# Attention and two gated MLPs on one core: a leaky rectifier in the weight conversion, and another order of the stages

## The chip, the cores and the metric

The kernel runs on one core of a Trainium2 chip. The time is that of one execution on the device, in microseconds, and what counts is the median of several runs. The profile is one execution recorded by the hardware; its own time stands beside it.

## The reference

The inputs are drawn as float32, but the weights and activations must keep nearly float32 accuracy. There are four batches of 12 heads, 448 positions and 64 features.

```
q, k   = rmsnorm(q) * g_q, rmsnorm(k) * g_k
attn   = softmax(q @ k.T / 8) @ v                 # per head
x      = attn, heads side by side                 # 1792 x 768
x      = ((x @ w_a) * (x @ w_b)) @ w_out          # 768 -> 1536 -> 768
h      = x @ w2_in                                # 768 -> 2048
g      = max(h, 0) + alpha * min(h, 0)            # alpha: one per column
out    = g @ w2_out                               # 2048 -> 768
```

## The kernel before

The work is split by batch and by stage. For each batch b there is the attention, and four stages: `a` (both products with `w_a` and `w_b`, 24 blocks of 18 matmuls), `y` (with `w_out`, 12 blocks), `h` (with `w2_in`, 16 blocks) and `o` (with `w2_out`, 24 blocks of 12 matmuls). All matmuls of a stage are 128x128 by 128x448 in float16. A number is carried as two float16 halves, a high and a low part, and three products are added, which gives 18 matmuls for six tiles (`prod`).

The order of the 16 stages is one written-out list, `stages` (L584). Attention of batch 0 runs alone, in float32, ahead of everything. Attention of batches 1 to 3 is cut into 21 steps each (`att_steps`): a step takes two blocks of query rows through scores, softmax (L417, L434), the split of the probabilities into halves (L477, L478) and a transposing DMA, and every 3.5 steps the product with v. The dictionary `RATE` (L883) says how many steps are laid between the blocks of a stage; whatever of batch b is still missing ahead of stage `a` of b is done there (`while done < ...`).

The weights come as pairs of 32-bit words of float64 numbers. Each block of weights is used once per batch. On its first use a block is loaded raw (`w_load`, L618), turned to float32 (`w_convert`), given a scale by a power of two from the sum of its squares (`w_scale`, `total`, `power`), split into halves (`w_split`, L684 and L685) and written to a scratch area in HBM (L688); later uses read it from there (L614). There are 76 such conversions: 24 in a, 12 in y, 16 in h, 24 in o. The list `STEPS` (L692) says how many blocks each of the four operations runs ahead of the block being multiplied.

`w_convert` works on the high words: ScalarE writes their absolute value times 2^-112 (L633), VectorE shifts the bits left by 3 (L634), puts the sign bit back (L637) and adds the top bits of the low word (L640); for `o` the inverse scale of `h` is multiplied in (L646). `w_scale` takes the squares (L666), sums them over the partitions by a small matmul with ones (the tile `tot`) and makes the scale.

Stage `h` evacuates a block as Relu(ps * cg) and Relu(-ps * cg) on ScalarE (L830, L831), adds alpha times the second (L832), copies to float16 (L836) and takes the rest as the low half (L837). Stages `a` and `y` do their own split (L739, L740) right away if the next stage is of the same batch; otherwise it is done piece by piece between the blocks of the following stages (`after`, `tasks`).

All activations live in a pool of 35 slots of one size. DMAs are issued on SyncE's queue (SP) in program order. A scheduler lays out the instructions of each engine from their order in the program and their dependences; a few are pinned by `keep_in_program_order`.

Of the kernel before, what the change touches and what calls it, by code (L numbers as in the profile page):

```python
# [8 lines left out]
F32 = mybir.dt.float32  # L9
F16 = mybir.dt.float16  # L10
# [3 lines left out]
AF = mybir.ActivationFunctionType  # L14
ALU = mybir.AluOpType
# [4 lines left out]
def attention_gated_mlps_kernel(  # L20
# [15 lines left out]
    nc = tc.nc  # L36
    B, H, S, D = q.shape
    DM, DF = w_a.shape
    DF2 = w2_in.shape[1]
    KD, KF, KF2 = DM // 128, DF // 128, DF2 // 128  # L40
    NP = H // 2
    NI = S // 64
    KB = 4
    KP = S // KB
    SLOTS = 35

    const = ctx.enter_context(tc.tile_pool(name="const", bufs=1))
    acts = ctx.enter_context(tc.tile_pool(name="acts", bufs=1))
# [5 lines left out]
    ob_p = ctx.enter_context(tc.tile_pool(name="ob", bufs=2))  # L54
    in_p = ctx.enter_context(tc.tile_pool(name="in", bufs=2))
    one_p = ctx.enter_context(tc.tile_pool(name="one", bufs=1))
    two_p = ctx.enter_context(tc.tile_pool(name="two", bufs=2))
    sm_p = ctx.enter_context(tc.tile_pool(name="sm", bufs=4))
# [6 lines left out]
    def slot(name):  # L65

        return slot_p.tile([128, 2, S], F16, tag="slot", name=name)
# [8 lines left out]
    kT0 = [kT0[:, i] for i in range(2)]  # L76
    kd0 = acts.tile([128, 2 * KB * D], F32, name="kd0")
    k16 = acts.tile([KP, 2, 2 * KB, 2, D], F16, name="k16")
    p16 = [acts.tile([128, 2, KB, 128], F16, name=f"p16_{i}") for i in range(3)]
    stat = [acts.tile([128, 2, NI + 2 * KB], F32, name=f"stat{i}") for i in range(2)]  # L80

    ident = const.tile([128, 128], F32, name="ident")
# [7 lines left out]
    gi = const.tile([128, 1], F32, name="gi")  # L90
    esc = const.tile([128, 1], F32, name="esc")
    al = const.tile([128, KF2], F32, name="al")
    alb = const.tile([128, KF2], F32, name="alb")
    cg = const.tile([128, 1], F32, name="cg")
    icg = const.tile([128, 1], F32, name="icg")
    ncg = const.tile([128, 1], F32, name="ncg")
    ssv = const.tile([KP, B, NP], F32, name="ssv")
    ssab = const.tile([128, 2, KF], F32, name="ssab")
    sx, ix, sab, iab, sy, iy, cum = [
# [12 lines left out]
    def power(total, s, i):  # L112


        n = total.shape[1]
        h = sm_p.tile([128, 4], I32, tag="pw", name="pw")[:, 0:n]
        nc.vector.tensor_scalar(
            h, total.bitcast(I32), 1, 0x7F800000, op0=ALU.logical_shift_right, op1=ALU.bitwise_and
        )
        nc.vector.tensor_scalar(  # L120
            s.bitcast(I32), h, -1.0, float(205 << 23), op0=ALU.mult, op1=ALU.add
        )
        nc.vector.tensor_scalar(i.bitcast(I32), h, 1.0, float(49 << 23), op0=ALU.mult, op1=ALU.add)

    def total(cols, n, groups=1):

        ps = ps_x.tile([128, 512], F32, tag="x", name="tot")
        p = cols.shape[0]
        mm(ps[:, 0:n], ones[:p], cols, True, True)
        if n == groups:  # L130
            return ps[:, 0:n]
        t = sm_p.tile([128, 4], F32, tag="tot", name="tots")[:, 0:groups]
        nc.vector.reduce_sum(
            out=t, in_=ps[:, 0:n].rearrange("p (g k) -> p g k", g=groups), axis=AX.X
        )
        return t
# [24 lines left out]
    def setup2():  # L161
        nc.gpsimd.dma_start(out=gbc, in_=g_q.rearrange("(o d) -> o d", o=1).broadcast_to([128, D]))
        nc.gpsimd.dma_start(out=gkb, in_=g_k.rearrange("(o d) -> o d", o=1).broadcast_to([128, D]))
        nc.gpsimd.dma_start(out=al, in_=alpha.rearrange("(f p) -> p f", p=128))
        nc.gpsimd.tensor_scalar(al, al, -1.0, None, op0=ALU.mult)

    def setup3():
        tc.keep_in_program_order(
# [15 lines left out]
    def setup4():  # L184

        q = sm_p.tile([128, KF2], F32, tag="al2", name="al2")
        nc.vector.tensor_tensor(q, al, al, op=ALU.mult)
        m = sm_p.tile([128, 1], F32, tag="alm", name="alm")
        nc.vector.tensor_reduce(out=m, in_=q, axis=AX.X, op=ALU.max)
        t = total(m, 1)  # L190
        one = sm_p.tile([128, 1], F32, tag="alm", name="alo")
        nc.vector.tensor_scalar(one, t, 1.0, None, op0=ALU.max)
        power(one, cg, icg)
        nc.vector.tensor_scalar(cg, cg, 2.0 ** -31, None, op0=ALU.mult)
        nc.vector.tensor_scalar(ncg, cg, -1.0, None, op0=ALU.mult)
        nc.vector.tensor_scalar(icg, icg, 2.0 ** 31, None, op0=ALU.mult)


# [160 lines left out]
        d["qT"], d["kT"] = qT, kT  # L359

    def load_vn(b, p):
        vn = one_p.tile([KP, 2, KB, D], F32, tag="vn", name="vn")
        nc.sync.dma_start(
            out=vn, in_=v[b, 2 * p:2 * p + 2].rearrange("h (p i) d -> p h i d", i=KB)
        )
        return vn
# [151 lines left out]
    X, Y, AB, G = {}, {}, {}, {}  # L518
# [62 lines left out]
            yield fin  # L581


    stages = "a0 y0 a1 y1 h0 o0 h1 o1 a2 y2 h2 a3 o2 y3 h3 o3".split()  # L584

    CHAINS = {"a": (2 * KF, 1, KD), "y": (KD, 2, KF // 2), "h": (KF2, 1, KD), "o": (KD, 4, KF2 // 4)}

    GROUP = {"a": 2, "y": 1, "h": 2, "o": 1}
# [16 lines left out]
    def size(kind):  # L605
        return CHAINS[kind][2] * 128
# [17 lines left out]
    def w_convert(u):  # L624
        if u not in raws:
            return
        kind, n, part = stream[u]
        raw = raws.pop(u)
        pair = raw.bitcast(I32).rearrange("p (n t) -> p n t", t=2)
        lo, hi = pair[:, :, 0], pair[:, :, 1]  # L630
        t = wf_p.tile([128, 768], F32, tag="wf", name="wf")[:, 0:size(kind)]
        ti = t.bitcast(I32)
        nc.scalar.activation(out=t, in_=hi.bitcast(F32), func=AF.Abs, scale=2.0 ** -112)  # L633
        i = nc.vector.tensor_scalar(ti, ti, 3, None, op0=ALU.logical_shift_left)  # L634
        if u == 0:
            tc.keep_in_program_order(i)
        nc.vector.scalar_tensor_tensor(  # L637
            out=ti, in0=hi, scalar=-0x80000000, in1=ti, op0=ALU.bitwise_and, op1=ALU.bitwise_or
        )
        nc.vector.scalar_tensor_tensor(  # L640
            out=ti, in0=lo, scalar=29, in1=ti, op0=ALU.logical_shift_right, op1=ALU.bitwise_or
        )
        if kind == "o":
            k = CHAINS["o"][2]
            t3 = t.rearrange("p (k f) -> p k f", f=128)
            nc.vector.tensor_tensor(  # L646
                t3, t3,
                inv["h"][:, part * k:(part + 1) * k].unsqueeze(2).to_broadcast([128, k, 128]),
                op=ALU.mult,
            )  # L650
        wf[u] = t

    def w_scale(u):

        kind, n, part = stream[u]
        if u not in wf:
            return
        _, parts, _ = CHAINS[kind]
        chains = GROUP[kind]
        if part < parts - 1 or n % chains < chains - 1:  # L660
            return
        us = range(u - parts * chains + 1, u + 1)
        ss = sm_p.tile([128, 4], F32, tag="ss", name="ss")[:, 0:len(us)]
        sc = sm_p.tile([128, 2], F32, tag="sc", name="sc")[:, 0:chains]
        for i, x in enumerate(us):
            nc.scalar.activation(  # L666
                out=junk(768, size(kind)), in_=wf[x], func=AF.Square, accum_out=ss[:, i:i + 1]
            )
        power(total(ss, len(us), chains), sc, inv[kind][:, n - chains + 1:n + 1])
        for x in us:  # L670
            scales[x] = sc[:, (x - us[0]) // parts:(x - us[0]) // parts + 1]

# [2 lines left out]
    def junk(width, n):  # L675
        return one_p.tile([128, width], BF16, tag="junk", name="junk")[:, 0:n]
# [12 lines left out]
        w16[u] = w  # L689


    STEPS = [(w_load, 9), (w_convert, 7), (w_scale, 7), (w_split, 3)]  # L692
    AGAIN = [(w_load, 4)]
    cur = [0]
    seen = set()
# [38 lines left out]
    def tmp():  # L734
        return tmp_p.tile([128, S], F32, tag="t", name="t")

    def split(t, s, name):
        x = slot(name)
        nc.scalar.activation(out=x[:, 0], in_=t, func=AF.Copy, scale=s)  # L739
        nc.vector.scalar_tensor_tensor(  # L740
            out=x[:, 1], in0=t, scalar=s, in1=x[:, 0], op0=ALU.mult, op1=ALU.subtract
        )
        return x
# [77 lines left out]
    def stage_h(b):  # L821
        for f in range(KF2):
            yield
            ps = new_ps()[:, 0:S]
            hw = unit()
            for kk in range(KD):
                prod(ps, hw, kk, Y[b, kk], kk == 0, kk == KD - 1)
            next_w()
            t, t2 = tmp(), tmp()
            nc.scalar.activation(out=t, in_=ps, func=AF.Relu, scale=cg)  # L830
            nc.scalar.activation(out=t2, in_=ps, func=AF.Relu, scale=ncg)  # L831
            nc.vector.scalar_tensor_tensor(  # L832
                out=t, in0=t2, scalar=al[:, f:f + 1], in1=t, op0=ALU.mult, op1=ALU.add
            )
            G[b, f] = g = slot(f"g{b}_{f}")
            nc.vector.tensor_copy(g[:, 0], t)  # L836
            nc.vector.tensor_tensor(g[:, 1], t, g[:, 0], op=ALU.subtract)  # L837
        for kk in range(KD):
            Y.pop((b, kk))

# [39 lines left out]
            G.pop((b, f))  # L880


    RATE = {"a0": 15.5, "y0": 8, "a1": 8, "y1": 4, "h0": 3, "o0": 3, "h1": 5, "o1": 5, "a2": 9, "y2": 6, "h2": 9}  # L883

    if True:
        load_qk(0)
# [17 lines left out]
        n, done = 0, 0  # L904
# [62 lines left out]
```

## Time and profile before

| | us |
|---|---|
| median of 3 runs | 1339.32 (1336.44 to 1340.88) |
| profiled execution | 1339.62 |
| its span | 1337.8 |
| mean granted clock of TensorE | 0.945 of full |

The stages stand in the span as follows, by the first and last matmul of each: attention of batch 0 alone up to 134.1; a0 to 282.0; y0 310.6 to 375.3; a1 376.7 to 479.2; y1 489.8 to 536.0; h0 536.8 to 598.6; o0 601.4 to 694.1; h1 to 758.5; o1 to 823.4; a2 825.5 to 921.9; y2 927.7 to 973.6; h2 977.1 to 1033.3; a3 to 1115.0; o2 to 1172.1; y3 1173.8 to 1214.8; h3 1218.3 to 1274.8; o3 to 1331.4.

A row of the windows view gives, for one stretch, the busy time of each engine with the number of its instructions, then the granted clock of TensorE as a share of full speed, the mean busy share of the 16 DMA engines, and GB/s.

### The profile page before, as it was taken

What the parts mean: (1) busy time and instruction counts of PE and PEld (TensorE: products, weight loads), DVE (VectorE), ACT (ScalarE), POOL (GpSimd) and SP (SyncE); (2) the same over time, 40 slices, a digit from 0 to 9 for tenths busy, and PEclk for the clock granted to TensorE, in tenths of its full rate; (3) what the DMA queues carried; (4) which work ended last, traced back from release to release, by engine and by line L of the source; (5) the groups of instructions that cost most, each with busy time, mean ns of one, the idle gap of its engine ahead of it and who ended that gap; (6) DMA issues with size and microseconds to landing.
All of it is one profiled execution on the core that took longest, in us unless ns stands there. A gap on an engine that the chain in (4) does not pass through costs nothing. (4 is left out here: it accounts for less than half of the span.)

```text
span 1337.8 us, 18305 instructions
## 1 busy us (share of the span) xinstructions
PE 1203.4 (90%) x6574; PEld 611.7 (46%) x6574; DVE 779.2 (58%) x1639; ACT 735.2 (55%) x1480; POOL 12.6 (1%) x33
## 2 busy tenths in 40 slices
PE   6697887667898989988889999998999999999998
PEld 4353343333344545443445554554545555544554
DVE  6788889788888476999968833334045113003510
ACT  6698788778775577976755634444133113013310
POOL 1000000000000000000000000000000000000000
PEclk9798898877898989998999999998999999999999
DMA  4536999997999956967888667765423433543333
GB/s 106 187 103 184 248 260 256 236 252 203 246 259 268 245 144 194 250 200 214 237 222 208 142 158 200 173 158 120 115 95 119 118 112 104 150 125 95 106 117 91
DMA packets 324491, 234.67 MB, mean 175 GB/s; under 512 B 190992, under 2 KB 297744, under 8 KB 324400
## 3 DMA queue, kind: packets, MB, share of 16 engines
q1 hardware_dynamic: 324288, 233.43, 65.8%
q8 instruction: 52, 0.85, 0.3%
q0 software_dynamic: 112, 0.07, 0.1%
q14 instruction: 39, 0.32, 0.1%
HBM read 155.79 MB, written 32.24 MB: 141 GB/s over the span
## 5 line engine op out<-in xcount | busy, mean ns | idle before, releaser
L110 PEld LDWEIGHTS <-w 128*128 128x128 f16 x4896 | 480.8, 100 | 519.7 <-issue 71.0
L110 PE MATMUL p<-x,w 128*128 128x448 f16 x1728 | 347.0, 361 | 16.6 <-DVE w L685 9.6
L110 PE MATMUL p<-g,w 128*128 128x448 f16 x1152 | 232.8, 361 | 15.6 <-ACT w L684 11.6
L110 PE MATMUL p<-y,w 128*128 128x448 f16 x1152 | 224.6, 356 | 3.9 <-ACT y L739 3.6
L110 PE MATMUL p<-ab,w 128*128 128x448 f16 x864 | 172.7, 360 | 6.7 <-ACT ab L739 4.2
L110 PE MATMUL s<-kT,qT 128*64 128x448 f16 (+1 forms) x588 | 109.2, 416 | 26.8 <-ACT pf L434 19.5
L417 DVE TENSOR_REDUCE nm<-s 128x2 f32<-128x896 f32 x84 | 91.2, 1085 | 35.6 <-PE s L110 35.1
L478 DVE SCALAR_TENSOR_TENSOR p<-pf,ri,p 128x448 f16<-128x448 f32 x126 | 83.3, 680 | 42.1 <-ACT p L477 41.9
L477 ACT ACTIVATE p<-pf,ri 128x448 f16<-128x448 f32 x126 | 80.3, 662 | 37.7 <-DMA pT<-p 32.9
L434 ACT ACTIVATE pf<-s,nm,esc 128x448 f32<-128x448 f32 x126 | 90.0, 718 | 2.7 <-DVE p L478 1.0
L761 DVE SCALAR_TENSOR_TENSOR ab<-p,inv_a,t 128x448 f32<-128x448 f32 x48 | 32.6, 679 | 94.0 <-PE p L110 93.7
L857 DVE TENSOR_SCALAR ob<-p,cum 112x512 f32<-112x512 f32 x24 | 18.0, 749 | 116.8 <-PE p L855 108.1
L848 ACT ACTIVATE t<-p,inv_o 128x448 f32<-128x448 f32 x24 | 25.6, 1067 | 107.3 <-PE p L110 107.3
L633 ACT ACTIVATE wf<-raw 128x768 f32<-128x768 f32 (+1 forms) x76 | 63.0, 831 | 37.3 <-DMA raw<-in_moe_w_out_dram 21.9
L830 ACT ACTIVATE t<-p,cg 128x448 f32<-128x448 f32 x64 | 40.3, 629 | 76.2 <-PE p L110 73.6
L832 DVE SCALAR_TENSOR_TENSOR t<-t,al 128x448 f32<-128x448 f32 x64 | 43.6, 681 | 56.1 <-ACT t L831 56.1
L685 DVE SCALAR_TENSOR_TENSOR w<-wf,sc,w 128x768 f16<-128x768 f32 (+1 forms) x76 | 70.2, 926 | 0.3 <-ACT w L684 0.3
L764 ACT ACTIVATE junk<-ab 128x448 bf16<-128x448 f32 x48 | 27.4, 572 | 75.5 <-DVE ab L761 73.2
L666 ACT ACTIVATE junk<-wf 128x768 bf16<-128x768 f32 (+1 forms) x76 | 58.8, 773 | 15.6 <-DVE wf L646 8.9
L684 ACT ACTIVATE w<-wf,sc 128x768 f16<-128x768 f32 (+1 forms) x76 | 63.2, 860 | 6.1 <-DVE sc L120 6.1
L637 DVE SCALAR_TENSOR_TENSOR wf<-raw,wf 128x768 int32<-128x768 int32 (+1 forms) x76 | 65.8, 866 | 0.2
L640 DVE SCALAR_TENSOR_TENSOR wf<-raw,wf 128x768 int32<-128x768 int32 (+1 forms) x76 | 65.8, 866 | 0.2
(134 smaller groups left out, 1080.3 us busy)
## 6 DMA issues: line engine op xcount, KB each, us to landing
w<-sc_a SPq DMA_DIRECT2D x72, 384.0 KB, 3.3
w<-sc_h SPq DMA_DIRECT2D x48, 384.0 KB, 3.1
w<-sc_o SPq DMA_DIRECT2D x72, 256.0 KB, 3.0
w<-sc_y SPq DMA_DIRECT2D x36, 384.0 KB, 3.1
raw<-in_moe_w_in_dram SPq DMA_DIRECT2D x16, 768.0 KB, 6.1
raw<-in_moe_w_out_dram SPq DMA_DIRECT2D x24, 512.0 KB, 3.9
raw<-in_moe_w_a_dram SPq DMA_DIRECT2D x12, 768.0 KB, 5.7
raw<-in_moe_w_b_dram SPq DMA_DIRECT2D x12, 768.0 KB, 5.6
```

The source lines that it names most:

```text
L110: nc.tensor.matmul(out=o, lhsT=a, rhs=b, start=first, stop=last)
L417: nc.vector.tensor_reduce(out=nm, in_=ps[:, :, 0:S], axis=AX.X, op=ALU.max, negate=True)
L434: nc.scalar.activation(out=pf, in_=ps[:, j, 0:S], func=AF.Exp, bias=nm[:, j:j + 1], scale=scale[j], accum_out=su[:, j:j + 1],)
L477: nc.scalar.activation(out=t[:, 0, :, 0:KP], in_=pf, func=AF.Copy, scale=r)
L478: nc.vector.scalar_tensor_tensor(out=t[:, 1, :, 0:KP], in0=pf, scalar=r, in1=t[:, 0, :, 0:KP], op0=ALU.mult, op1=ALU.subtract,)
L633: nc.scalar.activation(out=t, in_=hi.bitcast(F32), func=AF.Abs, scale=2.0 ** -112)
L637: nc.vector.scalar_tensor_tensor(out=ti, in0=hi, scalar=-0x80000000, in1=ti, op0=ALU.bitwise_and, op1=ALU.bitwise_or)
L640: nc.vector.scalar_tensor_tensor(out=ti, in0=lo, scalar=29, in1=ti, op0=ALU.logical_shift_right, op1=ALU.bitwise_or)
L666: nc.scalar.activation(out=junk(768, size(kind)), in_=wf[x], func=AF.Square, accum_out=ss[:, i:i + 1])
L684: nc.scalar.activation(out=w[:, 0], in_=t, func=AF.Copy, scale=s)
L685: nc.vector.scalar_tensor_tensor(out=w[:, 1], in0=t, scalar=s, in1=w[:, 0], op0=ALU.mult, op1=ALU.subtract)
L832: nc.vector.scalar_tensor_tensor(out=t, in0=t2, scalar=al[:, f:f + 1], in1=t, op0=ALU.mult, op1=ALU.add)
```

## The change

- `w_convert`: the function on ScalarE is a leaky rectifier (Prelu) with slope -(2^32) for negative inputs in place of Abs. A negative number comes out positive with its exponent raised by 32; the shift by 3 moves that bit into the sign. The instruction L637 goes.
- The squares of a block are taken at the end of `w_convert`; `w_scale` keeps the total and the scale. `STEPS` goes from 9, 7, 7, 3 blocks ahead to 10, 8, 6, 3.
- The order of the stages has `a0 y0 h0 o0` first, then the others; `RATE` is changed to match.
- Stage `h`: one Relu(-ps), then alpha' * that + ps on VectorE with alpha' = 1 - alpha, then the split that stages a and y use, with the scale cg. `setup2` and `setup4` prepare alpha' instead of -alpha and drop the column `ncg`; one instruction of `setup4` is pinned.
- There are four `p16` tiles instead of three; the loads of v for its norm (`load_vn`) take their buffer from the pool of the output tiles (two buffers) instead of one of their own.

```diff
-    p16 = [acts.tile([128, 2, KB, 128], F16, name=f"p16_{i}") for i in range(3)]
+    p16 = [acts.tile([128, 2, KB, 128], F16, name=f"p16_{i}") for i in range(4)]
...
-        nc.gpsimd.tensor_scalar(al, al, -1.0, None, op0=ALU.mult)
...
-        nc.vector.tensor_tensor(q, al, al, op=ALU.mult)
+        tc.keep_in_program_order(nc.vector.tensor_tensor(q, al, al, op=ALU.mult))
...
-        nc.vector.tensor_scalar(ncg, cg, -1.0, None, op0=ALU.mult)
+        nc.vector.tensor_scalar(al, al, -1.0, 1.0, op0=ALU.mult, op1=ALU.add)
...
-        vn = one_p.tile([KP, 2, KB, D], F32, tag="vn", name="vn")
+        vn = ob_p.tile([KP, 2, KB, D], F32, tag="ob", name="vn")
...
-    stages = "a0 y0 a1 y1 h0 o0 h1 o1 a2 y2 h2 a3 o2 y3 h3 o3".split()
+    stages = "a0 y0 h0 o0 a1 y1 a2 h1 o1 y2 a3 h2 y3 o2 h3 o3".split()
...
-        nc.scalar.activation(out=t, in_=hi.bitcast(F32), func=AF.Abs, scale=2.0 ** -112)
+        nc.scalar.activation(
+            out=t, in_=hi.bitcast(F32), func=AF.Prelu, scale=2.0 ** -112, alpha=-(2.0 ** 32)
+        )
         i = nc.vector.tensor_scalar(ti, ti, 3, None, op0=ALU.logical_shift_left)
...
-        nc.vector.scalar_tensor_tensor(
-            out=ti, in0=hi, scalar=-0x80000000, in1=ti, op0=ALU.bitwise_and, op1=ALU.bitwise_or
-        )
...
         wf[u] = t
+        _, parts, _ = CHAINS[kind]
+        j = (n * parts + part) % (parts * GROUP[kind])
+        if j == 0:
+            sums[0] = sm_p.tile([128, 4], F32, tag="ss", name="ss")
+        nc.scalar.activation(
+            out=junk(768, size(kind)), in_=t, func=AF.Square, accum_out=sums[0][:, j:j + 1]
+        )
+        if j == parts * GROUP[kind] - 1:
+            squares[u] = sums[0][:, 0:j + 1]
...
-        for i, x in enumerate(us):
-            nc.scalar.activation(
-                out=junk(768, size(kind)), in_=wf[x], func=AF.Square, accum_out=ss[:, i:i + 1]
-            )
-        power(total(ss, len(us), chains), sc, inv[kind][:, n - chains + 1:n + 1])
+        iv = inv[kind][:, n - chains + 1:n + 1]
+        power(total(squares.pop(u), len(us), chains), sc, iv)
...
-    STEPS = [(w_load, 9), (w_convert, 7), (w_scale, 7), (w_split, 3)]
+    STEPS = [(w_load, 10), (w_convert, 8), (w_scale, 6), (w_split, 3)]
...
-            t, t2 = tmp(), tmp()
-            nc.scalar.activation(out=t, in_=ps, func=AF.Relu, scale=cg)
-            nc.scalar.activation(out=t2, in_=ps, func=AF.Relu, scale=ncg)
+            t = tmp()
+            nc.scalar.activation(out=t, in_=ps, func=AF.Relu, scale=-1.0)
             nc.vector.scalar_tensor_tensor(
-                out=t, in0=t2, scalar=al[:, f:f + 1], in1=t, op0=ALU.mult, op1=ALU.add
+                out=t, in0=t, scalar=al[:, f:f + 1], in1=ps, op0=ALU.mult, op1=ALU.add
             )
-            G[b, f] = g = slot(f"g{b}_{f}")
-            nc.vector.tensor_copy(g[:, 0], t)
-            nc.vector.tensor_tensor(g[:, 1], t, g[:, 0], op=ALU.subtract)
+            G[b, f] = split(t, cg, f"g{b}_{f}")
...
-    RATE = {"a0": 15.5, "y0": 8, "a1": 8, "y1": 4, "h0": 3, "o0": 3, "h1": 5, "o1": 5, "a2": 9, "y2": 6, "h2": 9}
+    RATE = {"a0": 4, "y0": 5, "h0": 4, "o0": 8, "a1": 14, "y1": 7, "a2": 4, "h1": 4, "o1": 8, "y2": 6}
```

## Rows read from the trace of the kernel before

**Rows 1.** The page's first part: busy time, share of the span, instructions.
```profile
PE 1203.4 (90%) x6574; PEld 611.7 (46%) x6574; DVE 779.2 (58%) x1639; ACT 735.2 (55%) x1480; POOL 12.6 (1%) x33
```

**Rows 2.** Windows: five stretches from 134.1 us on, then a2 and a3 alone.
```profile
134.10:376.70 242.60, 189.59 (x1017) 89.76 (x1015) 207.07 (x416) 195.59 (x396) 0.83 (x1) 0.86 0.97 243
376.70:536.40 159.70, 150.80 (x853) 75.88 (x854) 108.47 (x225) 105.47 (x222) 2.24 (x4) 0.96 0.87 220
536.40:694.90 158.50, 138.27 (x711) 67.71 (x709) 146.76 (x299) 116.52 (x229) 2.02 (x3) 0.94 0.79 220
694.90:977.10 282.20, 273.33 (x1567) 138.69 (x1567) 123.85 (x243) 125.49 (x256) 0.62 (x4) 0.99 0.66 162
977.10:1337.80 360.70, 351.58 (x1856) 183.04 (x1855) 87.78 (x152) 85.83 (x147) 0.92 (x5) 0.99 0.38 112
824.00:921.90 97.90, 97.47 (x576) 49.02 (x571) 34.98 (x62) 43.82 (x102) 0.00 (x0) 1.00 0.61 149
1033.10:1115.00 81.90, 81.90 (x435) 42.37 (x433) 9.23 (x14) 16.14 (x36) 0.00 (x0) 1.00 0.38 110
```

**Rows 3.** Windows of line L478 alone (VectorE's busy time, count): attention's second halves.
```profile
134.10:376.70 242.60, 30.00 (x46) 0.86 0.97 243
376.70:536.40 159.70, 17.31 (x26) 0.96 0.87 220
536.40:694.90 158.50, 9.25 (x14) 0.94 0.79 220
...
824.00:921.90 97.90, 10.67 (x16) 1.00 0.61 149
```

**Rows 4.** Windows of line L637 alone: the sign pass of the conversions.
```profile
134.10:376.70 242.60, 27.64 (x30) 0.86 0.97 243
...
536.40:694.90 158.50, 22.09 (x30) 0.94 0.79 220
```

**Rows 5.** The chain that ended last: start us, us, what; 824 us to the end.
```profile
874.95 0.88 PE s L110 x8
875.82 2.27 PE x L110 x24
...
908.29 6.92 PE p L110 x36
...
927.72 19.55 PE p L110 x90
...
949.66 23.95 PE p L110 x126
...
977.07 139.46 PE p L110 x728
...
1173.97 40.88 PE p L110 x216
...
1218.31 67.83 PE p L110 x348
```

**Rows 6.** Groups by line: busy us, mean ns of one, idle before and releasers.
```profile
L685 DVE SCALAR_TENSOR_TENSOR w<-wf,sc,w 128x768 f16<-128x768 f32 (+1 forms) x76 | 70.2, 926 | 0.3 <-ACT w L684 0.3
...
L684 ACT ACTIVATE w<-wf,sc 128x768 f16<-128x768 f32 (+1 forms) x76 | 63.2, 860 | 6.1 <-DVE sc L120 6.1
L633 ACT ACTIVATE wf<-raw 128x768 f32<-128x768 f32 (+1 forms) x76 | 63.0, 831 | 37.3 <-DMA raw<-in_moe_w_out_dram 21.9 <-DMA raw<-in_moe_w_a_dram 5.6 <-DMA raw<-in_moe_w_b_dram 4.2
L666 ACT ACTIVATE junk<-wf 128x768 bf16<-128x768 f32 (+1 forms) x76 | 58.8, 773 | 15.6 <-DVE wf L646 8.9 <-DVE wf L640 3.0 <-DVE ri L471 2.5
...
L831 ACT ACTIVATE t<-p,ncg 128x448 f32<-128x448 f32 x64 | 40.1, 627 | 2.3 <-DVE t L832 2.3
...
L836 DVE CAST g<-t 128x448 f16<-128x448 f32 x64 | 25.0, 390 | 1.3
```

**Rows 7.** Waits of TensorE: engine, line, waited for, us, times, longest.
```profile
PE tot L110 <- ACT junk L666: 18.9, 11, 4.7
```

**Rows 8.** Groups by line: the only load of a function table.
```profile
L237 ACT ACT_TABLE_LOAD x1 | 1.3, 1283 | 0.7 <-PEq L951 0.7
```

More of the change, by code (lines that the diff above doesn't have):

```diff
@@ L92, in attention_gated_mlps_kernel @@
     al = const.tile([128, KF2], F32, name="al")
-    alb = const.tile([128, KF2], F32, name="alb")
     cg = const.tile([128, 1], F32, name="cg")
     icg = const.tile([128, 1], F32, name="icg")
-    ncg = const.tile([128, 1], F32, name="ncg")
     ssv = const.tile([KP, B, NP], F32, name="ssv")
@@ L651, in w_convert @@
         wf[u] = t
+        _, parts, _ = CHAINS[kind]
[7 more added lines that the diff above has]
+            squares[u] = sums[0][:, 0:j + 1]
+    sums, squares = [None], {}
     def w_scale(u):
+        if u not in squares:
+            return
         kind, n, part = stream[u]
-        if u not in wf:
-            return
         _, parts, _ = CHAINS[kind]
         chains = GROUP[kind]
-        if part < parts - 1 or n % chains < chains - 1:
-            return
         us = range(u - parts * chains + 1, u + 1)
-        ss = sm_p.tile([128, 4], F32, tag="ss", name="ss")[:, 0:len(us)]
         sc = sm_p.tile([128, 2], F32, tag="sc", name="sc")[:, 0:chains]
-        for i, x in enumerate(us):
-            nc.scalar.activation(
-                out=junk(768, size(kind)), in_=wf[x], func=AF.Square, accum_out=ss[:, i:i + 1]
-            )
-        power(total(ss, len(us), chains), sc, inv[kind][:, n - chains + 1:n + 1])
+        iv = inv[kind][:, n - chains + 1:n + 1]
+        power(total(squares.pop(u), len(us), chains), sc, iv)
         for x in us:
```

## The prediction

> **What bounds the kernel now.** I read the line of busy shares first [rows 1]: TensorE is 90% busy, VectorE 58%, ScalarE 55%. These are means over unlike stretches, so I cut the span at the ends of the stages (found in the timeline of TensorE) and read each stretch [rows 2]. Two kinds show. From 694.9 us on TensorE is busy over 96% at full clock, and the last third is a chain of back-to-back matmuls [rows 5]: one y stage, 216 matmuls, takes 40.88 us, or 0.189 us each. One batch has 24x18 + 12x18 + 16x18 + 24x12 = 1224 such matmuls, so TensorE needs 231.7 us a batch and no less.
>
> The other kind is the stretch with a0 and y0 (134.1 to 376.7) and that with h0 and o0 (536.4 to 694.9): 401.1 us, in which TensorE has 231.7 us of batch 0's matmuls and its share of attention. There its clock was granted at 0.86 and 0.94 of full, since it keeps running dry. These stretches hold 30 + 30 of the 76 weight conversions [rows 4], and 23 + 7 of the 63 attention steps of batches 1 to 3 (two L478 passes to a step, [rows 3]). VectorE is busy 207.07 + 146.76 = 353.8 us, or 88% of them (93% in the second); ScalarE 195.59 + 116.52 = 312.1 us, or 78%; the DMA engines 0.97 and 0.79. So the conversions bound these 401 us, by VectorE most of all, and the matmuls bound the rest. The whole can gain only in the 401 us and at the seams between stages.
>
> **The change part by part.**
>
> *The leaky rectifier.* It puts the sign in place in the ScalarE pass, and the VectorE pass L637 goes: 27.64 + 22.09 = 49.7 us in the two stretches [rows 4]. The ScalarE pass keeps its place and shape (L633, 0.831 us mean); I take the same time for the new function. Its bounds are the cheapest and dearest ScalarE passes of that tile, 0.773 (L666) and 0.860 us (L684) [rows 6], about -4 to +2 us over 68 conversions.
>
> *Shorter third-stage evacuation.* One ScalarE pass (L831, 0.627 us) is replaced by the first half of a split of the same size: nothing gained. Of three VectorE passes the middle one (L836, 0.390 us) goes: 16 x 0.390 = 6.2 us in h0 [rows 6]. In h1 to h3 VectorE idles beside TensorE, so it is worth nothing there. PSUM is now held until a VectorE pass has read it, not two ScalarE passes: with three buffers and 3.4 us of matmuls a block this hides; if not, it is under 0.7 us a block in h0, 11 us at the very worst.
>
> *Scale totals moved.* The squares go into the conversion step, the total comes one unit later. TensorE stood 18.9 us, 11 times, at the total's matmul waiting for the square [rows 7]; all of it lies where conversions run. In its place the square may hold ScalarE's queue until VectorE's two passes of its own unit are done. I count no gain; it supports that the stretches stay as full as before.
>
> *Order of stages and RATE.* The first four stages are now a0 y0 h0 o0, with 4 + 5 + 4 + 8 = 21 attention steps (all of batch 1) in place of 30, and with 68 conversions in place of 60 (8 instead of 7 are done ahead, none is left between). Raw loads and scratch writes of h and o are issued on SP's queue right behind those of y, the reloads for a1 and y1 later: the same transfers in another order, the conversions' share dealt with below. What a step costs is a2 less a3 [rows 2]: 43.82 - 16.14 = 27.7 us of ScalarE, 25.8 of VectorE, 0.61x97.9 - 0.38x81.9 = 28.6 of DMA, over 8 steps [rows 3]: 3.5, 3.2 and 3.6 us. A conversion is 63.0 + 58.8 + 63.2 = 185 us of ScalarE over 76, 2.43 us [rows 6]. So the new four stages need
> - ScalarE 312.1 - 9x3.46 + 8x2.43 = 300.4 us;
> - VectorE 353.8 - 49.7 - 6.2 - 9x3.2 + 8 conversions of at most three passes of 0.926 (L685) = 291 us;
> - DMA 0.97x242.6 + 0.79x158.5 = 360.5 us, less 9x3.6, plus 8 x 3.3 (the second stretch's 125.2 us less 7 steps, over 30 conversions) = 355 us;
> - TensorE 231.7 + 21 x 1.53 + two seams of 3.5 = 271 us (a step: 0.88 us of scores and 2.27 us of values for every 3.5 steps, [rows 5]).
>
> ScalarE is now the fuller of the two that convert. At the fullness that the fuller one reached before, 353.8/401.1 = 88%, that is 300.4/0.882 = 340.6 us. Bounds: 271 us (TensorE), and 355/0.97 = 366 us, if the DMA share of the first stretch means full queues. I take 340.6: the second stretch was filled to 93% by an engine at a DMA share of 0.79, and packets' times grow when more are in flight, so 0.97 is no proof of a bound.
>
> Elsewhere the stages move between stretches:
> - Up to 134.1 us: one conversion more, seven L637 passes less, one memset more (about 0.5 us each); VectorE is not the last there. No change; -4 to +3.
> - a1 y1, before 376.7 to 536.4 = 159.7 us with 13 steps, now 21: 8 x 1.53 = +12.2, so 171.9. Its conversions leave; what that frees I leave out (0 to -9).
> - h1 o1 a2 y2, before 694.9 to 977.1 = 282.2 us with about 20 steps, now 21 in the order a2 h1 o1 y2: +1.5. The seam a2 to y2, 915.21 to 927.72, goes but for 0.9 us of scores (y1's results wait in a2 and a2's in h1 and o1): -11.6. The seam y2 to h2, 973.61 to 977.07: -3.5 [rows 5]. That is 268.6.
> - The last six stages, 360.7 us: the seam y3 to h3, 1214.85 to 1218.31, goes (-3.5). New: in y3 the slots needed are 16 (h2's results) + 12 (a3's) + 3 + 6 = 37 of 35, so the last two evacuations wait for y3's last block, 0 to 36x0.189 = 6.8 us; y3 is followed by o2, which has its input, so I take 2. That is 359.2.
> - The fourth p16 buffer and the second buffer for the v loads shorten waits of ScalarE and of SP's queue. Where those engines bound nothing this is worth nothing; in the first stages it is inside the 88%.
>
> Sum: 134.1 + 340.6 + 171.9 + 268.6 + 359.2 = 1274.4 us of span, and 1.8 us around it (1339.62 less 1337.8): **1276 us**. The profiled execution is 0.3 us above the median, so the two need no correction.
>
> **The rivals.**
> *A: the conversions nearly vanish behind TensorE.* For: the stretch 376.7 to 536.4 ran at 159.7 us for 122.6 us of matmuls and 13 x 1.53 of attention, 1.12 times TensorE's need. Against: it had only nine conversions. 271 x 1.12 = 304 us in place of 340.6: 1240 us.
> *B: DMA bounds the first four stages.* For: 0.97 over 242.6 us, in which neither VectorE (85%) nor ScalarE (81%) was full. Against: the second stretch, as above, where an engine filled up long before the queues. 366 us: 1302 us.
> *C: the leaky rectifier shares no function table with the exponential, and every change between them loads one.* Only one load stands in the whole trace, 1.283 us [rows 8]: all functions used now share a table, but this one isn't among them. With 21 steps between 68 conversions there would be 42 to 136 loads; 89 loads add 114 us to ScalarE: (300.4 + 114)/0.882 = 470 us, and the total 1405 us. It decides from some 44 loads on (63 us lost, 0.882 x 63 = 56 us of ScalarE): slower than before. Against: nothing in the trace; that such a simple function is kept apart is merely unlikely.
> The Trainium skill, page "ScalarE: Activation LUTs", section "Table sets: the hidden batching unit", says that cheap functions stand in every set as filler and names relu and abs; the leaky one isn't in its list. By its section "What ACT_TABLE_LOAD costs" a change of set costs about 2.66 us with the drain; the load of 1.283 us in the trace agrees with that page's 1283 ns, and no run here yet shows the drain. By that price 89 changes would be 237 us.
> *D: slots.* In h1 the pool would hold 12 + 6 + 16 and two or three of batch 3's: 36 of 35. If batch 3's attention is held back until o1 frees them, some 6 steps run exposed before a3, at the 134.1/24 = 5.6 us that a step took in the first stretch alone: about +25 us, 1301 us.
>
> **How the numbers follow.** Forecast 0.62, A 0.12, B 0.17, C 0.06, D 0.03. The forecast's own range is 1250 to 1305. From 1235 to 1322 leaves out C, the far side of A, and a case of B in which the first stages come to over 387 us: about 2 in 10. Within 0.3% (1335 to 1343, about what a measurement of this kernel can tell from no change) needs first stages of 400 us: 0.04, from B's tail. Slower: C, and 0.03 from B and D together: 0.09. Faster: 0.87.
>
> **What would show it.** Right: batch 0's attention still ends at about 134 us; o0's last matmul comes near 475 us, with ScalarE and VectorE both near 300 us between; a1 and y1 take about 172 us; no seam between a2 and its successor; matmuls without a break from then on. Wrong: table loads beside L633 (C); TensorE waiting for raw loads or ScalarE's conversion waiting for them, with the DMA share at 0.97 and both engines under 80% (B); gaps on TensorE in h1 or y3 (D). The forecast fails most easily in the 88%: each point of it is 3.9 us.

## The result, and the profile after

The changed kernel takes 1287.09 us (median of 4 runs, 1283.99 to 1288.14), against 1337.88 us (1334.43 to 1340.88) in runs taken beside it: a ratio of 0.9617, 95% interval 0.9586 to 0.9648. The forecast was 1276 us. The profiled execution took 1286.1 us for a span of 1283.9 us.

The page's busy line answers to [rows 1]. VectorE lost 69.6 us and 139 instructions; ScalarE kept its 735 us; TensorE is at 92%.

```profile
PE 1177.9 (92%) x6574; PEld 604.0 (47%) x6574; DVE 709.6 (55%) x1500; ACT 734.5 (57%) x1480; POOL 9.8 (1%) x32
```

The windows of the changed kernel, cut at the ends of its stages (columns as in [rows 2]: start and end, length, busy time and count of PE, PEld, DVE, ACT, POOL, granted clock, DMA share, GB/s). The rows are: up to batch 0's last values; a0 y0 h0 o0; a1 y1; a2 h1 o1 y2; the last six stages.

```profile
0.00:124.00 124.00, 97.56 (x589) 55.96 (x590) 104.58 (x310) 110.04 (x243) 5.68 (x16) 0.94 0.64 168
124.00:465.20 341.20, 296.48 (x1616) 147.04 (x1615) 295.12 (x609) 291.52 (x577) 1.79 (x4) 0.94 1.00 272
465.20:652.40 187.20, 163.56 (x964) 80.73 (x965) 118.53 (x253) 119.63 (x263) 0.19 (x1) 0.95 0.87 203
652.40:928.30 275.90, 271.68 (x1548) 137.94 (x1548) 113.39 (x206) 124.42 (x252) 0.76 (x4) 0.99 0.62 154
928.30:1283.90 355.60, 348.57 (x1859) 182.33 (x1857) 77.98 (x124) 88.87 (x150) 1.34 (x7) 1.00 0.39 115
```

Read the lengths against the forecast's five terms:

| Stretch | Forecast | Measured | Off by |
|---|---|---|---|
| up to batch 0's last values | 134.1 | 124.0 | -10.1 |
| a0 y0 h0 o0 | 340.6 | 341.2 | +0.6 |
| a1 y1 | 171.9 | 187.2 | +15.3 |
| a2 h1 o1 y2 | 268.6 | 275.9 | +7.3 |
| last six stages | 359.2 | 355.6 | -3.6 |
| sum | 1274.4 | 1283.9 | +9.5 |

So the size of the total is partly luck: misses of -14 and +23 us stand behind an error of 9.5. The other 1.4 us are the time around the span (2.2 us, forecast 1.8) and the median above the profiled execution (1.0).

The attention steps lie as intended, but the planner ran two ahead. The same windows for line L475 (L478 before; columns as in [rows 3], two passes a step) show 23 and 21 steps in the second and third stretch, where 21 and 21 were forecast:

```profile
124.00:465.20 341.20, 29.53 (x46) 0.94 1.00 272
465.20:652.40 187.20, 28.11 (x42) 0.95 0.87 203
```

The groups of the changed kernel that answer to [rows 6] and [rows 8] (busy us, mean ns of one, then idle before it). The first is the leaky rectifier's pass (L633 before), the second stage h's ScalarE pass (L831 before), the third the one load of a function table:

```profile
L631 ACT ACTIVATE wf<-raw 128x768 f32<-128x768 f32 (+1 forms) x76 | 63.2, 835 | 28.7 <-DMA raw<-in_moe_w_out_dram 8.8 <-DMA raw<-in_moe_w_in_dram 7.5 <-DMA raw<-in_moe_w_a_dram 4.5
...
L832 ACT ACTIVATE t<-p 128x448 f32<-128x448 f32 x64 | 34.6, 541 | 54.3 <-PE p L108 54.1
...
L234 ACT ACT_TABLE_LOAD x1 | 1.3, 1283 | 0.7 <-PEq L950 0.7
```

The leaky pass costs 835 ns where the absolute value cost 831, and there is still one table load: rival C is dead. The 54 us before L832 are idle time behind TensorE and cost nothing.

The seams late in the kernel are gone. In the chain that ended last (start us, us, what), only a short norm and a total's pair of matmuls stand between long blocks of stage matmuls:

```profile
929.40 82.85 PE p L108 x438
1012.25 0.03 issue
1012.29 0.39 PE tot L108 x2
1012.68 93.84 PE p L108 x496
1106.52 0.95 PE norm L108 x5
```

### The profile page after: what moved, and what is told of

Its sections match the earlier page's. It is cut to its first block, busy times and chain, and to the rows that moved or that the text cites. A ratio compares the mean times of both kernels' runs of the same rounds, so it can differ in the third digit from the quotient of the medians.

```text
span 1283.9 us, 18197 instructions
## 1 busy us (share of the span) xinstructions
PE 1177.9 (92%) x6574; PEld 604.0 (47%) x6574; DVE 709.6 (55%) x1500; ACT 734.5 (57%) x1480; POOL 9.8 (1%) x32
## 5 line engine op out<-in xcount | busy, mean ns | idle before, releaser
L108 PE MATMUL p<-x,w 128*128 128x448 f16 x1728 | 339.7, 356 | 10.1 <-ACT t L760 6.7
L108 PE MATMUL s<-kT,qT 128*64 128x448 f16 (+1 forms) x588 | 105.5, 408 | 32.4 <-ACT pf L431 24.7
L414 DVE TENSOR_REDUCE nm<-s 128x2 f32<-128x896 f32 x84 | 91.0, 1084 | 36.2 <-PE s L108 35.9
L475 DVE SCALAR_TENSOR_TENSOR p<-pf,ri,p 128x448 f16<-128x448 f32 x126 | 83.2, 680 | 37.9 <-ACT p L474 37.9
L833 DVE SCALAR_TENSOR_TENSOR t<-t,al,p 128x448 f32<-128x448 f32 x64 | 43.4, 679 | 47.6 <-ACT t L832 47.6
L637 DVE SCALAR_TENSOR_TENSOR wf<-raw,wf 128x768 int32<-128x768 int32 (+1 forms) x76 | 65.8, 868 | 0.4
L832 ACT ACTIVATE t<-p 128x448 f32<-128x448 f32 x64 | 34.6, 541 | 54.3 <-PE p L108 54.1
L741 ACT ACTIVATE g<-t,cg 128x448 f16<-128x448 f32 x64 | 42.6, 666 | 34.7 <-DVE t L833 34.6
```

What stands on the lines that cost most here:

```text
L108: nc.tensor.matmul(out=o, lhsT=a, rhs=b, start=first, stop=last)
L414: nc.vector.tensor_reduce(out=nm, in_=ps[:, :, 0:S], axis=AX.X, op=ALU.max, negate=True)
L475: nc.vector.scalar_tensor_tensor(out=t[:, 1, :, 0:KP], in0=pf, scalar=r, in1=t[:, 0, :, 0:KP], op0=ALU.mult, op1=ALU.subtract,)
L637: nc.vector.scalar_tensor_tensor(out=ti, in0=lo, scalar=29, in1=ti, op0=ALU.logical_shift_right, op1=ALU.bitwise_or)
L833: nc.vector.scalar_tensor_tensor(out=t, in0=t, scalar=al[:, f:f + 1], in1=ps, op0=ALU.mult, op1=ALU.add)
```

## The experiments

Times are medians, ratios are to the kernel before, run beside them on the same chip, with a 95% interval in brackets; the changed kernel stands at 0.9617. The kernel before came to 1337 to 1342 us in these comparisons, so a difference of two medians from different comparisons can be off by some 3 us. Each of the edits is made to the changed kernel unless it says otherwise.

### One cause at a time, on the first four stages

**The old order back.**
```diff
-    stages = "a0 y0 h0 o0 a1 y1 a2 h1 o1 y2 a3 h2 y3 o2 h3 o3".split()
+    stages = "a0 y0 a1 y1 h0 o0 h1 o1 a2 y2 h2 a3 o2 y3 h3 o3".split()
...
-    RATE = {"a0": 4, "y0": 5, "h0": 4, "o0": 8, "a1": 14, ...
+    RATE = {"a0": 15.5, "y0": 8, "a1": 8, "y1": 4, "h0": 3, ...
```


> The changed kernel with the stages and RATE of before; all else kept. Theory (the first four stages are as long as the fuller of VectorE and ScalarE needs at 88%): in the stretches with a0 y0 and h0 o0 VectorE falls by 50 + 6 us to 298 and ScalarE keeps 312, so the 401 us become 354; with batch 0 done 16 us earlier that is 1338 - 47 - 16 = 1275 us, no slower than the new order. Rival (the DMA queues, at 0.97, set a0 and y0 in the old order): those 243 us stay, only h0 o0 gains some 30 us: 1338 - 30 - 16 = 1292 us or more.

1287.2 us, 0.9586 [0.9566, 0.9606]: the same as the changed kernel, within the intervals, and between its theory (1275) and its rival (1292). The most visible part of the change, the order, is worth nothing that can be measured here. The windows of its profiled execution (the slowest of its runs, 1293.65 us), first a0 y0, then h0 o0:

```profile
125.60:349.40 223.80, 181.71 (x1004) 88.36 (x1004) 182.60 (x384) 188.26 (x388) 0.19 (x1) 0.89 1.06 259
...
507.50:650.70 143.20, 131.62 (x722) 65.93 (x721) 128.28 (x270) 116.80 (x234) 1.80 (x3) 0.98 0.94 255
```
Together 367.0 us where [rows 2] had 401.1: the stretches with conversions shrink in the old order too.

**The sign pass back.**
```diff
...
-            out=t, in_=hi.bitcast(F32), func=AF.Prelu, scale=2.0 ** -112, alpha=-(2.0 ** 32)
+        nc.scalar.activation(out=t, in_=hi.bitcast(F32), func=AF.Abs, scale=2.0 ** -112)
...
+        nc.vector.scalar_tensor_tensor(
+            out=ti, in0=hi, scalar=-0x80000000, in1=ti, op0=ALU.bitwise_and, op1=ALU.bitwise_or
+        )
```


> The changed kernel with Abs and the VectorE sign pass back: 76 more VectorE passes of 0.87 us, 67 of them in the first four stages (58 us). Theory: VectorE, at 300.5 of 347.5 us there, becomes the fuller engine, 358/0.88 = 407 us: total 1287 + 59 = 1346 us. Rival (DMA bounds these stages, its share is 1.00): up to 15 us lost, 1287 to 1302 us.

1323.67 us, 0.9868 [0.9845, 0.989]. The loss of some 36 us (34 by the ratios) lies between the theory and the rival. The window of the first four stages:

```profile
124.20:501.30 377.10, 303.04 (x1635) 148.57 (x1635) 347.49 (x683) 298.72 (x584) 3.11 (x4) 0.92 0.90 245
```
VectorE is now busy 92% of it, 52.4 us more than in the changed kernel, and the stretch is 35.9 us longer: 0.7 us for each us of VectorE. Over the whole kernel it is 36 us for 76 passes of some 66 us, or about 0.5 for each. The DMA share falls from 1.00 to 0.90, so here VectorE does lead.

**The leaky rectifier alone, on the kernel before.** The reverse of that edit, nothing else.

> The kernel before with only the leaky rectifier in place of Abs and the sign pass. Theory (VectorE's 50 us less in the two stretches give back about half, as the changed kernel in the old order showed, 12.6 and 15.5 us): 1338 - 28 = 1310 us, or 1295 if the plan of the first stretch changes with it. Rival (the gain needs the new order): 1325 to 1338 us.

1307.47 us, 0.9771 [0.9715, 0.9826]: some 31 us of the 51 come from this one part (23 to 38 by the interval), as its theory had it. Its windows of a0 y0 and h0 o0, 363.3 us together where [rows 2] had 401.1:

```profile
132.70:352.00 219.30, 181.30 (x1012) 86.83 (x1012) 182.45 (x383) 188.82 (x391) 0.89 (x1) 0.91 1.05 265
...
520.00:664.00 144.00, 131.10 (x720) 65.54 (x717) 132.90 (x287) 116.56 (x231) 1.55 (x3) 0.98 0.91 249
```
The two stretches give 37.8 us, and a1 y1 between them takes 168.0 us (352.0 to 520.0) where it took 159.7, so a part of the gain is lost again there.

**Less VectorE still: the low-word pass left out** (the weights lose their last three bits).
```diff
-        nc.vector.scalar_tensor_tensor(
-            out=ti, in0=lo, scalar=29, in1=ti, op0=ALU.logical_shift_right, op1=ALU.bitwise_or
-        )
```


> The changed kernel without the pass that adds the low word's bits (VectorE, 0.868 us, 67 times or 58 us in the first four stages); the weights lose their last three bits. Theory (VectorE sets the pace; putting a pass in cost 36 us): 1287 - 36 = 1251 us. Rival one (ScalarE, at 298 us, takes over at once): 1275 to 1285 us. Rival two (DMA): 1287 us.

1268.64 us, 0.9498 [0.9472, 0.9525]: 18.5 us less (16 by the ratios) for a pass of 65.8 us in all, or 0.3 us for each, between the theory and its first rival. Its window from batch 0's last values to o0's end:

```profile
124.20:454.00 329.80, 293.60 (x1628) 148.84 (x1628) 249.40 (x542) 291.27 (x579) 1.69 (x4) 0.95 1.05 284
```
VectorE is down to 76%, the stretch gave 11 us for 46 us less of VectorE, and the DMA share is 1.05.

**Less ScalarE: squares over an eighth of the weights** (so the scales are wrong).
```diff
-            out=junk(768, size(kind)), in_=t, func=AF.Square, accum_out=sums[0][:, j:j + 1]
+            out=junk(768, size(kind) // 8), in_=t[:, 0:size(kind) // 8], func=AF.Square, accum_out=...
```


> The changed kernel with the squares of each block taken over an eighth of its columns (the scale of the weights is made from a part of them): some 0.55 us of ScalarE less for each of 67 conversions, 37 us. Theory (ScalarE sets the pace beside VectorE): 1287 - 20 = 1267 us. Rival (VectorE or DMA alone): 1283 to 1287 us.

1281.56 us, 0.9587 [0.9559, 0.9614], not separable from the changed kernel. The window from the last values to o0:

```profile
118.30:459.00 340.70, 295.49 (x1622) 146.01 (x1622) 297.51 (x613) 264.75 (x579) 2.16 (x4) 0.95 1.02 274
```
ScalarE falls to 78% there (26.8 us less) and the stretch is no shorter (340.7 us for 341.2); it only starts and ends some 6 us earlier.

**More DMA: half of each raw block loaded again.**
```diff
+        x = one_p.tile([128, 3, 128], I64, tag="dup", name="dup")[:, 0:n // 256]
+        nc.sync.dma_start(out=x, in_=source(*key)[:, 0:n // 256])
```


> The changed kernel with half of every raw block loaded a second time into a tile that nothing reads (384 or 256 KB more for each of the 76 conversions, on the same queue). It leaves nothing out. Theory (the first four stages are set by the DMA queues, share 1.00): at the 270 GB/s of this stretch 43 x 1.45 + 24 x 0.97 = 86 us of transfers more, total 1355 to 1375 us. Rival (VectorE and ScalarE set them): 1287 to 1300 us.

1346.8 us, 1.0082 [1.0054, 1.0109]: slower than the kernel before, 60 us over the changed one, and somewhat short of what its theory gave.

```profile
139.40:527.00 387.60, 304.43 (x1622) 152.20 (x1621) 304.65 (x611) 296.14 (x578) 2.35 (x4) 0.88 1.01 284
```
The four stages take 46 us more with both engines' work nearly the same (VectorE 79%, ScalarE 76%); 15 us more go ahead of them. The DMA share stays at 1.01 while the bytes a second rise from 272 to 284 GB/s.

The run adds more than bytes, though. The second copies share one buffer, and each stands in SP's queue until the copy before it has landed. The queue's longest waits in this stretch (engine, line, waited for, us, times, longest), first in this run, then in the changed kernel:

```profile
SPq L617 <- DMA dup<-in_moe_w_out_dram: 67.4, 24, 5.4
SPq L617 <- DMA dup<-in_moe_w_in_dram: 45.8, 11, 6.7
...
SPq L615 <- DVE wf L637: 42.2, 25, 3.5
SPq L690 <- DVE w L687: 36.3, 18, 7.4
```
The queue stands 113.2 us at the copies. How much of the 46 us comes from the bytes and how much from the raw loads held behind them is not separated: a run with a buffer of its own for each copy is missing.

These runs agree on one picture: no single resource sets the time of these stages. Adding to VectorE costs much, taking from it gives less, and taking from ScalarE nothing that shows; adding transfers costs much too, with the queue's waits in the price.

### The second v buffer and the first stretch

**Only the second v buffer, on the kernel before.**
```diff
-        vn = one_p.tile([KP, 2, KB, D], F32, tag="vn", name="vn")
+        vn = ob_p.tile([KP, 2, KB, D], F32, tag="ob", name="vn")
```


> The kernel before with only the second buffer for these loads. Theory as in the run before: 1338 - 12 = 1326 us. Rival: 1336 to 1340 us.

1326.24 us, 0.9885 [0.9869, 0.9901]: 15 us gained by an edit that the prediction had put at nothing. In the profiled executions it is 13.0 us, 8.6 of them up to batch 0's last values (125.5 for 134.1). The issues on SP's queue in the kernel before (start us, us, engine, line, operation, tile, count):

```profile
25.80 11.48 SPq L363 DMA_DIRECT2D vn<-in_v_dram  x4
...
44.22 0.35 SPq L211 DMA_DIRECT2D qr<-in_q_dram  x1
```
and with two buffers:

```profile
27.59 2.71 SPq L363 DMA_DIRECT2D vn<-in_v_dram  x2
...
35.63 0.35 SPq L211 DMA_DIRECT2D qr<-in_q_dram  x1
```
Four loads into one buffer each wait until the one before has landed and ScalarE has read it, and the q and k of a later pair stand behind them in the same queue. TensorE's longest wait between 30 and 62 us shows it (engine, line, waited for, us, times, longest), in the kernel before:

```profile
PE p L324 <- DVE kd L277: 8.8, 1, 8.8
```
and with two buffers:

```profile
PE p L324 <- DVE kd L277: 1.7, 1, 1.7
```

**The single v buffer back, in the changed kernel** (the reverse).

> The changed kernel with the loads of v for its norm in one buffer again. Theory (the 16 us at batch 0's attention come from that buffer: SyncE's queue stood at the next such load until ScalarE had read the one before, and the q and k of the next pair were queued behind): batch 0's last values come at some 130 us in place of 117, total 1297 to 1301 us. Rival (they come from the conversions and the pinned instruction): 1287 to 1290 us.

1288.07 us, 0.9603 [0.9585, 0.9621]: no loss. The train of four loads is back, and TensorE stalls again, where the changed kernel has no such wait; the profile now names the gates' setup, which VectorE reached late. The queue and then the waits of this kernel in that stretch:

```profile
23.46 11.48 SPq L360 DMA_DIRECT2D vn<-in_v_dram  x4
...
40.51 0.35 SPq L208 DMA_DIRECT2D qr<-in_q_dram  x1
```
```profile
PE tot L108 <- DVE al L192: 9.1, 1, 9.1
PE p L321 <- DVE kd L274: 1.7, 1, 1.7
```
Its first window, up to batch 0's last values, is 2.8 us longer than in the changed kernel (126.8 for 124.0), not the 13 that were expected:

```profile
0.00:126.80 126.80, 96.40 (x574) 56.65 (x575) 100.37 (x302) 106.27 (x231) 5.72 (x16) 0.91 0.56 157
```
Its last o0 matmul ends 9 us later than in the changed kernel (473.7 for 464.4), y1's 5 us later (654.5 for 649.7), and at the end 1.6 us are left. So in the new order the time lost early is made good later; on the kernel before it was not. An equal total doesn't say that the stall is gone: the trace has one, and it is hidden.

**A pin of program order alone, on the kernel before** (the change has it too).
```diff
-        nc.vector.tensor_tensor(q, al, al, op=ALU.mult)
+        tc.keep_in_program_order(nc.vector.tensor_tensor(q, al, al, op=ALU.mult))
```


> The kernel before with only the product of alpha with itself (L187, VectorE) pinned to its place in the program. Theory (in the kernel before, VectorE stood 4.2 us at this instruction early on, and the late loads of q and k in SyncE's queue come from the plan that follows; any edit that moves it dissolves the stall at 45 to 54 us): batch 0 done at 118 to 121 us, total 1322 to 1327 us. Rival (only the second buffer or the cheaper conversion does it): 1336 to 1341 us.

1336.09 us, 0.9992 [0.9977, 1.0007]: no effect. Batch 0's last values come at 131.9 us, and the stall stays (same view):

```profile
PE p L324 <- DVE kd L277: 10.9, 1, 10.9
```

### The other parts

**Totals back in the scale step.**
```diff
-    STEPS = [(w_load, 10), (w_convert, 8), (w_scale, 6), (w_split, 3)]
+    STEPS = [(w_load, 9), (w_convert, 7), (w_scale, 7), (w_split, 3)]
```
with the squares moved from the conversion to the scale step.

> The changed kernel with the squares in the scale step again and 9, 7, 7, 3 blocks ahead. Theory (the first four stages hang on transfers, VectorE and ScalarE together, and TensorE's waits at the totals only shift): within 8 us of 1287. Rival (the earlier squares saved the 19 us that TensorE stood at the totals): 1300 to 1310 us.

1293.9 us, 0.9666 [0.962, 0.9712]. Up to 7 us, but the intervals overlap: not settled.

**Stage h's evacuation back.**
```diff
-            t = tmp()
-            nc.scalar.activation(out=t, in_=ps, func=AF.Relu, scale=-1.0)
+            t, t2 = tmp(), tmp()
+            nc.scalar.activation(out=t, in_=ps, func=AF.Relu, scale=cg)
+            nc.scalar.activation(out=t2, in_=ps, func=AF.Relu, scale=ncg)
...
```


> The changed kernel with the third stage's old evacuation (one VectorE pass of 0.39 us more per block, 6.2 us in h0). Theory: VectorE costs 0.3 to 0.6 us per us in the first stages: 1289 to 1291 us, and nothing in h1 to h3. Rival (PSUM held longer by the new form costs as much): 1283 to 1287 us.

1288.08 us, 0.9631 [0.9585, 0.9677]: nothing measurable.

**Attention spread more evenly over a1 and y1**, with a fifth p16 buffer.
```diff
-    RATE = {..., "a1": 14, "y1": 7, ...}
+    RATE = {..., "a1": 11, "y1": 10, ...}
```


> The changed kernel with RATE a1 11 and y1 10 in place of 14 and 7, and a fifth p16 tile. Theory (a1 is 15 us longer than its matmuls and steps because ScalarE's queue waits for transposes with attention packed densely): a1 shorter by 5 to 8 us, y1 longer by 5, the rest of the gain from the tile: 1281 to 1285 us. Rival (packing is not the cause): 1286 to 1290 us.

1285.86 us, 0.9612 [0.9569, 0.9655]: the same. a1 got 11 us shorter and y1 11 us longer; from a1's first matmul to y1's last it is 183.7 us in both kernels. So the steps are not packed too densely into a1, and a fifth p16 buffer gains nothing.

## Why the prediction came out near, and which of its steps failed

**The leaky rectifier** was rightly named as the part that gains, by VectorE's time in the stretches with conversions: -31 us alone, -36 by taking it out. Its pass costs what was assumed. The pass that goes was work for VectorE and also a link in the chain of each conversion; no run separates the two.

**The 88% of the first four stages.** The time was met (341.2 for 340.6), not the reading behind it. ScalarE came to 291.5 us (300.4 forecast), VectorE to 295.1 (291): both at about 86%, with the DMA share at 1.00. So VectorE, not ScalarE, was still the fuller of the two, and at the assumed 88.2% its work would have given 334.6 us: less work than forecast and a lower fullness cancelled, which is luck. The contents differ as well: the stretch holds 23 steps for 21, and 66 conversions for 68, by the passes of line L637 (windows, VectorE's busy time and count):

```profile
124.00:465.20 341.20, 56.38 (x66) 0.94 1.00 272
```
By the prediction's own prices these two nearly cancel for ScalarE (+6.9 and -4.9 us), so its sum was some 11 us too high for other reasons, which stay open. The DMA share was discounted as no proof of a bound, against rival B. The runs speak for its being part of the bound: with VectorE lightened further the share went to 1.05 and only 11 us came, and 46 us were lost when transfers were added, though there the queue's waits have a part. It isn't a wall at 1.00 either, since the bytes a second rose to 284. Rival B as priced (366 us) is 25 us too dear; rival A (304 us) is further off still.

**"Up to 134.1 us: ... No change; -4 to +3."** This step failed, outside its bounds: 124.0. So did, as a reason, what was said of the second buffer for the v loads: "Where those engines bound nothing this is worth nothing". SP's queue was indeed no bound; a load at its head, waiting for its one buffer, still held the q and k behind it. It is worth 15 us on the kernel before. In the changed kernel, as it happens, taking it out costs nothing at the end: the number was right there, the reason was not. What made this term 10.1 us shorter is not settled. Alone on the kernel before, the second buffer brings batch 0's last values from 134.1 to 125.5, the pin to 131.9 and the leaky rectifier to 132.7; but with the single buffer back the changed kernel still has them at 126.8. How these parts combine is open.

**"8 x 1.53 = +12.2" for a1 y1.** The price of the steps holds: TensorE is busy 163.6 us for 150.8 in [rows 2], +12.8 for eight more steps. What was left out is waiting. TensorE is idle 187.2 - 163.6 = 23.6 us, where [rows 2] gives 159.7 - 150.8 = 8.9 us: +14.7 of the +15.3 missed. TensorE's longest waits in the kernel before (376.7 to 536.4 us), then all its waits from 466 to 652 us in the changed kernel:

```profile
PE p L110 <- ACT t L758: 4.0, 1, 4.0
PE s L110 <- ACT pf L434: 3.5, 1, 3.5
...
PE s L108 <- ACT pf L431: 6.4, 3, 3.8
PE p L108 <- ACT t L760: 3.8, 2, 2.8
PE p L108 <- DVE ab L763: 3.1, 1, 3.1
PE tot L108 <- ACT junk L766: 2.0, 1, 2.0
PE x L108 <- DMA pT<-p: 1.9, 1, 1.9
PE s L108 <- DMA kT<-k: 1.8, 1, 1.8
PE s L108 <- ACT v L382: 1.5, 1, 1.5
```
Scores wait for the exponential that frees their PSUM (pf), and stage a's matmuls for its evacuations (t, ab). The wait for t was there before; the one for pf is 2.9 us longer, that for ab grew too, and attention's own transposes and copies (pT, kT, v) add 5.2 us that the kernel before did not have. Another 2.8 us lie at the very end, ahead of a2's norm. ScalarE is busy only 64% of the stretch. Shifting the steps between a1 and y1 left the same total; why these waits add up so is open.

**"The seam a2 to y2 ... -11.6", "The seam y2 to h2 ... -3.5".** The seams went, but TensorE's idle time in that stretch was only 282.2 - 273.3 = 8.9 us [rows 2], so 15.1 us could not be had. The two seams were read off the chain that ended last, and there the time between two pieces on TensorE went to other engines while TensorE worked on something else. The windows of the two seams in the kernel before:

```profile
915.20:927.70 12.50, 7.27 (x53) 3.86 (x53) 5.24 (x12) 6.15 (x14) 0.19 (x1) 0.92 0.81 163
973.60:977.10 3.50, 1.32 (x7) 0.52 (x6) 1.04 (x5) 1.96 (x4) 0.42 (x3) 0.97 0.35 112
```
TensorE is idle for 5.2 and 2.2 us in them; in the first it runs attention's scores and values and a2's own last block of 18 matmuls. Idle is now 275.9 - 271.7 = 4.2 us, 4.7 less; busy time 1.6 less. That the two seams could not be worth 15 us could have been read from the rows.

**Slots in y3 (+2), and rival D:** no such waits; the last six stages are 3.6 us shorter than forecast. **Totals and stage h:** no gain was put into the sum for either; taking stage h's part out shows none, and the totals may be worth up to 7 us.

**Where the 51 us come from.** The leaky rectifier is 31 to 36. On the kernel before, it and the second buffer alone gave 31 and 15 us, which would add up to 46 of the 54 us that the changed kernel gains in the old order. In the changed kernel the rest, 15 to 20 us, belongs to no single part: without the second buffer the changed kernel stays at 1288, without the new order at 1287, but with only the leaky rectifier it is 1307. That either of the two makes up for the other is argued from these three runs; a kernel that lacks both but keeps the totals and stage h was not run, so the totals' share in it is open. The fourth p16 buffer was never taken out, so its share is open as well.

## What to carry to other kernels

Several loads into one buffer hold all that stands behind them in an in-order queue, even if that queue and its engine are far from full: look at the order of issues before costing a buffer at nothing, and give an experiment's added loads enough buffers. Where two engines and the DMA are all near full, expect less than what relieving one frees: here about half, and about a quarter the second time. A seam on TensorE is worth its idle time and no more, and a gap between two of its pieces in the chain that ended last is not idle time until a window says so. A stage that gets more interleaved work pays in waits as well as in matmuls.

## What the runs showed of the hardware

Stage h's rectifier reads the same 128x448 block from PSUM as before, but with a constant as its scale instead of a column of 128 values: 541 ns instead of 627 [rows 6], 86 ns less. The Trainium skill, page "ScalarE: Activation LUTs", section "What ACT_TABLE_LOAD costs", puts a column operand at about 93 ns; the trace nearly agrees, with 86. The mean DMA share, which rival B had read as full at 0.97, went to 1.06 in these runs, and at 1.00 to 1.01 the rate still rose from 272 to 284 GB/s when more was queued.
